# Sliding-window attention and MLP on one core: tables made on GpSimd, mask tables made later, the last block written in column halves

## The chip, the cores and the metric

The kernel runs on 1 core of one Trainium2 chip. The metric is the device time of one execution in microseconds (us). The times given for a kernel are the median of several runs.

## The reference

Inputs are q, k and v of shape (8 batches, 8 heads, 576 positions, 64) in float32, a gain of 512 values, and two weight matrices of 512 x 2048 and 2048 x 512. Cut to what matters, the reference computes:

```python
scores = q @ k.T / sqrt(64)
rel = pos[:, None] - pos[None, :]
mask = (rel >= 0) & (rel < 128)                 # causal, window of 128
scores = where(mask, scores - slope[head] * rel, -1e9)
x = softmax(scores) @ v                         # heads side by side: (8, 576, 512)
xn = (x - mean(x)) / sqrt(var(x) + 1e-6) * g    # over the 512 columns
out = x + relu(xn @ w_ch1) @ w_ch2
```

A softmax row is not shifted by its maximum in the kernel; the sum of the exponentials comes from a column of ones beside v.

## The kernel before

**Blocks and chunks.** The 8 x 576 rows are cut into 36 blocks of 128 rows. Two batches make a period of 9 blocks; block 4 of a period holds the end of one batch and the start of the next, and block 5 follows it. Each block sees itself and the block before it. Blocks are gathered into chunks (`CHUNKS`, L249: 2, 3, 3 and then seven of 4) for the MLP.

**Attention of a block** (L483 to L767): q, k and v are loaded on SP's queue (L360, or L436 for pairs of blocks, the "spans" starting at blocks 0, 2, 5 and 7, L280); q and k are cast to 16 bits (L498, or L530 for a span); they are transposed on TensorE (L563, L538) and copied out (L571, L552, L550), and from block 12 on by a DMA transpose (L578). Scores are computed into the PSUM banks `sc` (L599), ScalarE takes exp (L647), and the result is multiplied by a mask table that holds exp(-slope * distance) or 0 (L654). For blocks under `BY_BIAS` = 6 there is no multiply: TensorE first adds the bias to the scores with 8 matmuls per block of a scaled identity `sid` and a distance table `dist_t` (L615, the Z tasks). Then probabilities times v (L671, the pv tasks), a reciprocal and a multiply (L688, L692), the statistics (L709, L714), `xs` (L720), and its transpose: on TensorE (L732, copied out at L740 or L742) for blocks under `X_BY_DMA` = 13, by DMA (L747) after.

**Tables.** The identity, `dist_t` in its three kinds (ordinary, the block with a batch border, the block after it) and the gain row are loaded on ScalarE's queue (L377, L381, L385). `sid` is made from the identity on VectorE (L403). The mask tables `mreg` (8 instructions of ScalarE, L410), `mmix` and `mnew` (4 copies and 3 memsets on GpSimd, L420 to L427) are made once, behind the pv of block 1 (`TABLE_AFTER`, L278, and L829).

**MLP of a chunk** (L769 to L825): 16 A tasks of 4 matmuls each (L781, as many columns as the chunk has rows), a relu after each on ScalarE or VectorE (L793, L791), and for each block 4 B tasks of 4 matmuls of 512 columns (L807), then `ot` = B * rstd + x (L815) and the store on SP's queue (L823).

**Weights.** Eight transfers of 512 columns or rows, issued on GpSimd's queue (L474 for w1, L476 for w2). `W_AFTER` (L463) says behind which cast each is issued: entry `at` stands for block at // 3, and at % 3 for its q, k or v cast (for a block of a span, always the v cast). The relu rows of 4 A tasks need one w1 quarter.

**What sets the order.** Everything is a task with a list of what it depends on, an urgency `v` (smaller first), the engines that could take it with an assumed duration on each, and, for TensorE's work, the PSUM banks. `Plan.run` (L100 to L220) plays this forward in Python with the assumed durations and writes out a fixed instruction order for each engine. A wait is met on the chip, but the order stays. `SLACK` (L281) is a time that the planner adds between an end on another engine and TensorE's use of it (first value under 30 us, second after, third behind weight transfers). `PICK` (L282) says per task and block which engines are allowed; where two are, an engine leaves the task to the other if that one would end sooner (L166). For the multiply the assumed durations are VectorE 0.69 and GpSimd 1.4 us (L658); for the cast of a span GpSimd 1.25, ScalarE 1.06 and VectorE 0.65 us (L531). Where TensorE would be idle in the first `WARM` = 26 us of the plan, small filler matmuls on zeros are emitted (L839); until then they hold the fourth of the four PSUM banks `fb`. `LEAD` shifts how far attention runs ahead of the MLP.

Of the kernel before, what the change touches and what calls it, by code (L numbers as in the profile page):

```python
# [13 lines left out]
ALU = mybir.AluOpType  # L14
# [32 lines left out]
class Plan:  # L47
# [7 lines left out]
    BEGIN = 0.75  # L55
    LANDING = {"DMA SP": (0.7, 1.3), "DMA ACT": (0.7, 1.3), "DMA POOL": (1.6, 1.4)}
    LAST_OF_RUN = 1.0

    def __init__(self):
        self.tasks, self.rings, self.banks, self.opens = [], [], {}, {}  # L60
# [6 lines left out]
    def add(self, name, eng, emit, deps=(), v=0.0, lat=None, acq=None, rel=None):  # L67
        if not isinstance(eng, dict):
            eng = dict([eng])
        if lat is None:  # L70
            lat = 0.2 if "PE" in eng else 0.05 + max(self.OVERLAP.get(e, 0.0) for e in eng)
        eng = {e: c - self.OVERLAP.get(e, 0.0) for e, c in eng.items()}
        t = Task(name, eng, emit, deps, v, lat, acq, rel)
        self.tasks.append(t)
        return t

# [5 lines left out]
        i.room = d.room = room  # L82
        return i, d

    SLACK = (0.2, 0.2, 0)

    def slack(self, t, when):

# [11 lines left out]
    def run(self):  # L100
# [15 lines left out]
        heap, n = [], 0  # L116
        for t in self.tasks:
            if t.left == 0:
                heap.append((self.BEGIN, n, t))
                n += 1  # L120
        for x in self.opens.values():
            heap.append((x, n, None))
# [25 lines left out]
        while left:  # L148
            while heap and heap[0][0] <= now + 1e-9:
                t = heapq.heappop(heap)[2]  # L150
# [8 lines left out]
            for e in engines:  # L159
# [3 lines left out]
                for t in avail[e]:  # L163
# [8 lines left out]
                    ok, b = bank(t)  # L172
# [4 lines left out]
                t, b = best  # L177
# [11 lines left out]
                if t.rel is not None:  # L189
                    waits[t.rel] -= 1  # L190
                    if waits[t.rel] == 0:
                        p, hb = held[t.rel]
# [31 lines left out]
def kernel(  # L224
# [21 lines left out]
    PERIOD = 2 * S // P  # L246
    CB = 4
    CH = CB * P
    CHUNKS = [2, 3, 3, 4, 4, 4, 4, 4, 4, 4]  # L249
    FIRST = [sum(CHUNKS[:c]) for c in range(len(CHUNKS))]  # L250
    CHUNK_OF = [c for c, n in enumerate(CHUNKS) for _ in range(n)]
    VD = D + 2
# [5 lines left out]
    def head_of(bank, slot):  # L258
        return 2 * (2 * (bank // 2) + slot) + bank % 2

    kk = np.arange(P)[:, None]
    cc = np.arange(2 * P)[None, :]
    qq = cc % P
    rel = np.where(cc < P, cc + P, cc - P) - kk
    valid = (rel >= 0) & (rel < window)
    tail = np.where(cc < P, qq < HALF, (kk >= HALF) | (qq < HALF))
    head = (cc >= P) | (kk >= HALF)
    dist = np.stack([np.where(m, rel, 16000) for m in (valid, valid & tail, valid & head)], 1).astype(np.float16)
    dist_dram = nc.inline_tensor(dist, name="dist")
    iden_dram = nc.inline_tensor(np.eye(P, dtype=np.float16), name="iden16")  # L270

    pool = ctx.enter_context(tc.tile_pool(name="sb", bufs=1))
    psum = ctx.enter_context(tc.tile_pool(name="ps", bufs=1, space=bass.MemoryType.PSUM))

    SPAN = 36.0
    LEAD = 1.5
    WARM = 26.0
    TABLE_AFTER = 1  # L278
    SPLIT = 6
    SPANS = [0, 2, 5, 7]  # L280
    SLACK = (0.1, 0.4, 0.5)  # L281
    PICK = {('xt', 0): 'ACT DVE', ('xt', 8): 'ACT', ('cv', 5): 'POOL ACT', ('cv', 0): 'POOL', ('ev', 8): 'DVE', ('ev', 1): 'DVE', ('mkb', 8): 'DVE', ('mkb', 3): 'POOL', ('mka', 2): 'DVE', ('mkb', 4): 'POOL', ('ev', 3): 'ACT', ('mka', 0): 'DVE', ('ck', 8): 'ACT', ('mkb', 0): 'POOL', ('cq', 5): 'POOL', ('ev', 5): 'DVE', ('ck', 2): 'POOL', ('ck', 7): 'POOL ACT', ('mkb', 6): 'DVE', ('mka', 5): 'DVE', ('cq', 6): 'POOL ACT', ('cq', 2): 'POOL ACT', ('xt', 6): 'ACT DVE', ('mka', 7): 'DVE', ('cq', 8): 'ACT', ('xt', 5): 'DVE', ('mka', 6): 'POOL', ('cv', 7): 'POOL ACT', ('cv', 3): 'POOL', ('xt', 3): 'ACT DVE', ('mka', 4): 'POOL', ('mka', 3): 'POOL', ('ev00', 4): 'DVE', ('cs1', 1): 'POOL', ('cs0', 0): 'POOL ACT', ('ev10', 3): 'DVE', ('xt', 2): 'ACT', ('cq', 3): 'POOL', ('cs0', 8): 'POOL ACT', ('ev01', 8): 'DVE', ('ev10', 8): 'ACT', ('ev11', 5): 'ACT', ('cs0', 2): 'POOL ACT', ('cq', 4): 'POOL', ('ev00', 8): 'DVE ACT', ('ev01', 0): 'ACT', ('cv', 8): 'ACT', ('ev11', 0): 'ACT', ('cv', 4): 'POOL', ('mkb', 5): 'POOL', ('ev01', 6): 'DVE', ('cv', 6): 'ACT', ('ev10', 5): 'DVE ACT', ('cs1', 4): 'POOL ACT', ('ev', 0): 'ACT', ('cv', 2): 'POOL ACT', ('ev00', 2): 'ACT', ('ev00', 7): 'ACT', ('ev10', 2): 'DVE'}  # L282
    BY_BIAS = 6
    MASK_AT = 6
    QK_BY_DMA = 12
    X_BY_DMA = 13

    plan = Plan()
    plan.SLACK = SLACK

    def sb(name, shape, dt):
        return pool.tile(shape, dt, tag=name, name=name)
# [47 lines left out]
    def av(i, stage=0.0):  # L340
        return (i / CB - LEAD) * SPAN + stage

# [31 lines left out]
    for t in vx.tiles:  # L374
        nc.vector.memset(t[:, :, D:VD], 1.0)

    d_iden = plan.transfer("iden", "ACT", 0.5, 0.15, 0.0, lambda e, b: nc.scalar.dma_start(out=iden, in_=iden_dram.ap()), (), -1e6)[1]  # L377
    d_dist = [
        plan.transfer(
            f"dist{n}", "ACT", 0.5, 0.25 * (k1 - k0), 0.0,  # L380
            lambda e, b, k0=k0, k1=k1: nc.scalar.dma_start(out=dist_t[:, k0:k1, :], in_=dist_dram.ap()[:, k0:k1, :]), deps, v,  # L381
        )[1]
        for n, k0, k1, deps, v in ((0, 0, 1, (), -9e5), (1, 1, 3, (), av(2, 0.0)))
    ]
    d_row = plan.transfer("g", "ACT", 0.5, 0.02, 0.0, lambda e, b: nc.scalar.dma_start(out=g_row[:, :], in_=moe_g_ln.unsqueeze(0)), (), -8e5)[1]  # L385

# [14 lines left out]
    for h in range(H):  # L401
        def emit(e, b, h=h):
            nc.vector.tensor_scalar(out=sid[:, h, :], in0=iden[:, :], scalar1=-float(slopes[h] / inv_sqrt_d), scalar2=None, op0=ALU.mult)  # L403
# [3 lines left out]
    for bank in range(4):  # L407
        for slot in range(2):
            def emit(e, b, bank=bank, slot=slot):
                nc.scalar.activation(  # L410
                    out=mreg[:, bank, slot, :], in_=dist_t[:, 0, :], func=AF.Exp,
                    scale=-float(slopes[head_of(bank, slot)]),
                )
            tm.append(add(f"mreg{bank}{slot}", ("ACT", 0.4), emit, [d_dist[0]], av(MASK_AT, 0.0)))
    tmix, tnew = [], []
    for dst, lst, name in ((mmix, tmix, "mmix"), (mnew, tnew, "mnew")):
        vv = av(MASK_AT, 0.0)
        for hb in range(2):
            def emit(e, b, dst=dst, hb=hb):
                nc.gpsimd.tensor_copy(dst[:, 2 * hb : 2 * hb + 2, :, :], mreg[:, 2 * hb : 2 * hb + 2, :, :])  # L420
            lst.append(add(f"{name}c{hb}", ("POOL", 1.2), emit, tm, vv))
    def z1(e, b):
        nc.gpsimd.memset(mmix[:, :, :, HALF:P], 0.0)
    def z2(e, b):
# [35 lines left out]
            load("v", v, v32, i, vl + 0.02),  # L460
        )

    W_AFTER = [11, 13, 14, 14, 17, 18, 18, 22]  # L463
    t_w = {}

    def weights(i, casts):
# [16 lines left out]
    def attention(i):  # L483
# [142 lines left out]
        for halves in ((0,), (1,)) if i < SPLIT else ((0, 1),):  # L626
            tag = "ab"[halves[0]] if i < SPLIT else ""
            acq = [(f"sc{hf}", f"S{i}{hf}") for hf in halves]
            part = len(halves) / 2
            z_ = []  # L630
            if bias:
                z_ = [add(f"Z{tag}{i}", ("PE", (0.87 if r else 0.46) * part), e_z(halves), t_sid + [d_dist[kind > 0]], av(i, 1.5 + 0.6 * halves[0]), acq=acq)]
            st_ = add(f"S{tag}{i}", ("PE", 0.19 + (0.45 if r else 0.23) * part), e_s(halves), z_ + qkt_done[i] + prev, av(i, 2.0 + 0.6 * halves[0]), acq=acq)
            qkt.reads(i, st_)
            if r:
                qkt.reads(i - 1, st_)
            for half in halves:
                s_[half] = st_
# [130 lines left out]
    def mlp(c):  # L769
# [26 lines left out]
            relu.append(r_)  # L796
        for j in range(nb):
            i = FIRST[c] + j
            key = f"B{i}"
            last = None  # L800
            for f0 in range(0, NFB, 4):
                vm = v0 + 16 * per + (4 * j + f0 / 4) * SPAN / 32

                def e_b(e, b, j=j, f0=f0, key=key):
                    pm = fb[plan.held[key][1]]
                    for f in range(f0, f0 + 4):
                        nc.tensor.matmul(  # L807
                            pm[:, :], ht[c][:, f, j * P : j * P + P], w2sb[:, f, :],
                            start=(f == 0), stop=(f == NFB - 1),
                        )  # L810
                last = add(f"{key}.{f0}", ("PE", 0.864), e_b, relu[f0 : f0 + 4] + [t_w[4 + f0 // 4][1], last], vm, acq=("fb", key))
                ht.reads(c, last)

            def e_o(e, b, i=i, j=j, key=key):
                nc.vector.scalar_tensor_tensor(  # L815
                    out=ot[i][:, :], in0=fb[plan.held[key][1]][:, :], scalar=rstd[c][:, j : j + 1],
                    in1=xb[i][:, :], op0=ALU.mult, op1=ALU.add,
                )
            o = add(f"o{i}", ("DVE", 0.75), e_o, [last, kept[c]], vm - 4.0, rel=key)
            ot.writes(i, o); rstd.reads(c, o); xb.reads(i, o)  # L820

            def e_d(e, b, i=i):
                nc.sync.dma_start(out=out_flat[i * P : i * P + P, :], in_=ot[i][:, :])  # L823
            t, d = plan.transfer(f"out{i}", "SP", 0.42, 0.8, 0.12, e_d, [o], vm - 4.0)
            ot.reads(i, d)  # L825

    for i in range(NBLK):
        attention(i)
        if i == TABLE_AFTER:  # L829
            for t in tm:  # L830
                t.deps.append(pv_done[i])
    for c in range(len(CHUNKS)):
        mlp(c)

# [45 lines left out]
```

The softmax here doesn't subtract the row's maximum and nothing guards it: scores larger than these inputs give would overflow.

## Time and profile before

| what | value |
|---|---|
| time, median of 7 runs | 324.61 us (323.83 to 325.96) |
| the profiled execution's own time | 324.12 us |
| its span, first to last instruction | 322.3 us |
| TensorE busy | 314.3 us, 2640 matmuls, of them 138 fillers |
| VectorE, ScalarE, GpSimd busy | 181.4, 162.6 and 79.7 us |
| granted TensorE clock | 1.00 over the whole span |
| moved by DMA | 51.91 MB |

The profile is that of one execution. "L781" is line 781 of the kernel. PE is TensorE's matmuls, PEld its weight loads, DVE VectorE, ACT ScalarE, POOL GpSimd, SP the engine that issues most DMAs; a q behind an engine's name is its queue of issuing instructions. In a timeline, a row gives the start, the time from there to the end of the last instruction merged into it, the engine, the line, the operation, what it writes and reads, and in square brackets how long the engine had been idle and what released it. Matmuls overlap in the pipeline, so the time that a matmul adds is read from the distance between starts, not from its duration.

### The profile page before, as it was taken

How to read it: one execution, taken by the hardware profiler on the slowest of the kernel's cores; microseconds unless marked ns; L12 is line 12 of the kernel's file. 1: busy time of each engine (PE TensorE's matmuls, PEld its weight loads, DVE VectorE, ACT ScalarE, POOL GpSimd, SP SyncE). 2: the span in 40 equal slices, each digit the busy share in tenths (PEclk: the TensorE clock that was granted, in tenths of full speed). 3: DMA queues.
4: the chain of work that ended last, by engine and by line, in shares of the span. 5: the costliest groups of instructions: out<-in, count | busy, mean ns of one | idle time of the engine just before them, and what ended most of it. 6: DMA issues, size and time to landing. Idle time of an engine off the chain costs nothing.

```text
span 322.3 us, 6669 instructions
## 1 busy us (share of the span) xinstructions
PE 314.3 (98%) x2640; PEld 171.9 (53%) x2640; DVE 181.4 (56%) x398; ACT 162.6 (50%) x264; POOL 79.7 (25%) x116
## 2 busy tenths in 40 slices
PE   8989999999999999999999999999999999999994
PEld 6877775556644554554454444444444444444441
DVE  1289189677610696695397496566756675321011
ACT  2798897134704950683277434752475247305500
POOL 2379272354202420620340260160000000000000
PEclk9999999999999999999999999999999999999999
DMA  8999999999999996999999899984420220011011
GB/s 203 237 214 217 244 200 214 215 200 268 224 198 260 206 189 132 243 218 208 177 221 197 179 169 254 229 164 116 114 49 18 83 82 18 17 67 65 0 66 65
DMA packets 151921, 51.91 MB, mean 161 GB/s; under 512 B 134737, under 2 KB 147281, under 8 KB 151890
## 3 DMA queue, kind: packets, MB, share of 16 engines
q1 hardware_dynamic: 147232, 47.07, 69.7%
q0 software_dynamic: 4224, 4.19, 7.8%
q8 instruction: 20, 0.33, 0.5%
q10 hardware_dynamic: 434, 0.23, 0.3%
q14 instruction: 11, 0.09, 0.1%
HBM read 36.93 MB, written 9.44 MB: 144 GB/s over the span
## 4 chain that ended last, share of the span: by engine, by line
PE 85%; DMA 5%; SPq 4%; DVE 3%; issue 1%; ACT 0%; POOL 0%; DVEq 0%; POOLq 0%
PE fb L807 38%; PE fb L781 37%; PE sc L599 5%; PE fb L671 4%; DMA w1sb<-in_moe_w_ch_dram 3%; SPq L360 3%; SPq L436 1%; DMA k<-in_k_dram 1%; DVE probs L654 1%; DVE st L709 1%; PE fb L732 1%; DVE xs L720 0%; PE fb L563 0%; DVE xb L692 0%; DVE xt L740 0%
## 5 line engine op out<-in xcount | busy, mean ns | idle before, releaser
L781 PE MATMUL fb<-xt,w1sb 128*128 128x512 f16 (+2 forms) x640 | 135.5, 358 | 0.7 <-DVE xt L740 0.3
L807 PE MATMUL fb<-w2sb,ht 128*128 128x512 f16 x576 | 132.5, 379 | 0.0
L793 ACT ACTIVATE ht<-fb 128x512 f16<-128x512 f32 (+2 forms) x142 | 78.9, 557 | 77.9 <-PE fb L781 76.6
L647 ACT ACTIVATE probs<-sc 128x1024 f16<-128x1024 f32 (+1 forms) x72 | 67.5, 976 | 42.8 <-PE sc L599 42.8
L781 PEld LDWEIGHTS <-w1sb 128*128 128x128 f16 x640 | 59.3, 98 | 54.9 <-issue 0.6
L807 PEld LDWEIGHTS <-ht 128*128 128x128 f16 x576 | 54.0, 98 | 60.7 <-issue 0.2
L815 DVE SCALAR_TENSOR_TENSOR ot<-fb,rstd,xb 128x512 f32<-128x512 f32 x36 | 27.0, 749 | 59.2 <-PE fb L807 52.2
L654 DVE TENSOR_TENSOR probs<-probs,mreg 128x1024 f16<-128x1024 f16 (+1 forms) x47 | 33.1, 712 | 20.7 <-ACT probs L647 20.5
L512 POOL CAST vx<-v 128x512 f16<-128x512 f32 x33 | 20.8, 633 | 87.4 <-PE fb L671 61.1
L498 POOL CAST qk<-q 128x512 f16<-128x512 f32 x28 | 19.3, 691 | 57.2 <-DMA qkt<-qk 46.7
L671 PEld LDWEIGHTS <-probs 128*128 128x128 f16 x544 | 24.4, 97 | 12.8 <-issue 1.3
L692 DVE TENSOR_TENSOR xb<-fb,rec 128x256 f16<-128x256 f32 x72 | 29.9, 421 | 1.7
L720 DVE SCALAR_TENSOR_TENSOR xs<-xb,mv,g_t 128x512 f16<-128x512 f16 x36 | 28.3, 787 | 2.8 <-DMA xt<-xs 1.9
L671 PE MATMUL fb<-vx,probs 128*128 128x65 f16 x544 | 27.2, 193 | 1.0 <-DVE qkt L550 0.9
L688 DVE RECIPROCAL rec<-fb 128x4 f32<-128x4 f32 x72 | 12.2, 175 | 24.9 <-PE fb L671 24.6
L709 DVE BATCH_NORM_STATS2 st<-xb 128x6 f32<-128x512 f16 x36 | 24.9, 692 | 1.0
L498 POOL CAST qk<-k 128x512 f16<-128x512 f32 x28 | 19.5, 698 | 6.9 <-DMA k<-in_k_dram 4.2
L599 PEld LDWEIGHTS <-qkt 64*128 64x128 f16 x544 | 15.3, 94 | 10.7 <-issue 9.1
L599 PE MATMUL sc<-qkt 64*128 64x128 f16 x288 | 19.6, 216 | 0.1
L791 DVE TENSOR_SCALAR ht<-fb 128x512 f16<-128x512 f32 (+2 forms) x18 | 10.8, 605 | 15.3 <-PE fb L781 14.5
L599 PE MATMUL sc<-qkt,qkt 64*128 64x128 f16 x256 | 18.3, 219 | 0.0
L839 PE MATMUL fb<-warm_t 128*128 128x128 f16 x138 | 11.1, 245 | 1.0 <-DVE warm_t L371 1.0
(47 smaller groups left out, 115.5 us busy)
## 6 DMA issues: line engine op xcount, KB each, us to landing
out_dram<-ot SPq DMA_DIRECT2D x36, 256.0 KB, 2.5
v<-in_v_dram SPq DMA_DIRECT2D x32, 256.0 KB, 4.9
q<-in_q_dram SPq DMA_DIRECT2D x24, 256.0 KB, 5.1
k<-in_k_dram SPq DMA_DIRECT2D x24, 256.0 KB, 4.9
qs<-in_q_dram SPq DMA_DIRECT2D x4, 512.0 KB, 6.1
ks<-in_k_dram SPq DMA_DIRECT2D x4, 512.0 KB, 7.9
w1sb<-in_moe_w_ch_dram POOLq DMA_DIRECT2D x4, 512.0 KB, 10.9
w2sb<-in_moe_w_ch_dram POOLq DMA_DIRECT2D x4, 512.0 KB, 8.8
```

What stands on the lines that cost most here:

```text
L498: en.tensor_copy(out=qk16[nrm[i]][:, a, :], in_=s)
L599: nc.tensor.matmul(scs[half][:, g, c0 : c0 + P], kt[rows, 1, hp, :], qkt[i][rows, 0, hp, :], start=not bias, stop=True, skip_group_check=True,
L647: nc.scalar.activation(out=o, in_=n_, func=AF.Exp, scale=inv_sqrt_d)
L654: en.tensor_tensor(out=pv, in0=pv, in1=mask[:, 2 * half : 2 * half + 2, :, lo:], op=ALU.mult)
L671: nc.tensor.matmul(pp[:, hh * (D + 1) : hh * (D + 1) + D + 1], probs[i][:, bank, slot, side * P : side * P + P], vx[i - 1 + side][:, h, 0 ...
L692: nc.vector.tensor_tensor(out=xb[i][:, 256 * half : 256 * half + 256].rearrange("p (h d) -> p h d", d=D), in0=pp[:, :, 0:D], in1=rec[2 * i ...
L709: nc.vector.bn_stats(out=st[i][:, :], in_=xb[i][:, :])
L720: nc.vector.scalar_tensor_tensor(out=xs[i][:, :], in0=xb[i][:, :], scalar=mv[c][:, j, 0:1], in1=g_t[:, :], op0=ALU.subtract, op1=ALU.mult,)
L781: nc.tensor.matmul(fb[b][:, 0:n_], w1sb[:, kb, f * P : f * P + P], xt[c][:, kb, 0:n_], start=(kb == 0), stop=(kb == NKB - 1),)
L793: nc.scalar.activation(out=ht[c][:, f, 0:n_], in_=src, func=AF.Relu)
L807: nc.tensor.matmul(pm[:, :], ht[c][:, f, j * P : j * P + P], w2sb[:, f, :], start=(f == 0), stop=(f == NFB - 1),)
L815: nc.vector.scalar_tensor_tensor(out=ot[i][:, :], in0=fb[plan.held[key][1]][:, :], scalar=rstd[c][:, j : j + 1], in1=xb[i][:, :], op0=ALU. ...
```

## The change

All of it is in one function and the planner above it.

1. The identity and `dist_t` are no longer loaded but made on GpSimd (memset, iota, affine_select, copies). The gain row is still loaded.
2. `mreg` is made behind the pv of block 3 instead of block 1, and `mmix` and `mnew` behind that of block 4.
3. `BY_BIAS` goes from 6 to 5: block 5 is masked by the multiply instead of the Z matmuls. `X_BY_DMA` goes from 13 to 14, so block 13's `xs` is transposed on TensorE instead of by DMA.
4. The last chunk of 4 blocks becomes one of 3 and one of 1. Block 35's B is done in two column halves, each in a PSUM bank, with its own `ot` instruction and store.
5. `W_AFTER`, `SPLIT`, `LEAD`, `WARM`, `SLACK` and `MASK_AT` get other values, `PICK` gets an entry for nearly every task of blocks 0 to 11, and `PRI` and `HOLD` are new: an amount added to a task's urgency, and an earliest time for it in the plan.

Of `PICK`, these entries matter below. The casts of the first span, `('cs0', 0)` and `('cs1', 0)`, go from "POOL ACT" (and GpSimd by default) to "POOL DVE". The multiplies of a block's two halves (`mka`, `mkb`) are allowed on GpSimd alone for block 5 (first half) and blocks 6, 8 and 11 (both halves): 7 instructions. Before, from block 6 on, only the first half of block 6 was; VectorE does all others.

```diff
-    SLACK = (0.2, 0.2, 0)
+    SLACK: tuple = (0, 0.4, 0)
...
-    CHUNKS = [2, 3, 3, 4, 4, 4, 4, 4, 4, 4]
+    CHUNKS = [2, 3, 3, 4, 4, 4, 4, 4, 4, 3, 1]
...
-    LEAD = 1.5
-    WARM = 26.0
-    TABLE_AFTER = 1
-    SPLIT = 6
+    LEAD = 1.7
+    WARM = 20.0
+    TABLE_AFTER = 3
+    MIX_AFTER = 4
+    SPLIT = 4
...
-    SLACK = (0.1, 0.4, 0.5)
+    SLACK = (0.1, 0.3, 0.4)
...
+    PRI = {'mka7': -7.4, 'T9': -24.7, 'k11.i': 0.8, 'v4.i': 5.2, 'B2.0': -1.2, 'v5.i': 8.4, 'Sa0': -9.2}
+    HOLD = {'S9': 59.97, 'Zb2': 14.76, 'rc1.3': 20.0, 'dist': 1.4, 'G': 4.27, 'ck9': 49.72, 'eT0.10': 8.66, 'rs2': 51.44, 'pva2': 19.78}
-    BY_BIAS = 6
-    MASK_AT = 6
+    BY_BIAS = 5
+    MASK_AT = 5
...
-    X_BY_DMA = 13
+    X_BY_DMA = 14
...
+    d_iden = pool_do("iden1", 0.2, [], -1e6, lambda en: en.memset(iden[:, :], 1.0))
+    d_iden = pool_do("iden2", 0.3, [d_iden], -9e5, keep(iden[:, :], iden[:, :], 0, 1, -1, 0.0, ALU.is_equal))
+    t = pool_do("dist", 0.35, [], -8e5, lambda en: en.iota(
+        dist_t[:, 0, :].rearrange("p (s c) -> p s c", s=2), pattern=[[-P, 2], [1, P]], base=P, channel_multiplier=-1,
+        allow_small_or_imprecise_dtypes=True,
+    ))
+    t = [
+        pool_do("dist00", 0.3, [t], -7e5, keep(dist_t[:, 0, 0:P], dist_t[:, 0, 0:P], -1, 1, -1, far)),
+        pool_do("dist01", 0.3, [t], -7e5, keep(dist_t[:, 0, P:], dist_t[:, 0, P:], 0, -1, 1, far)),
+    ]
+    d_dist = [t, [
+        pool_do("dist1", 0.35, t, av(2, -8.0), lambda en: en.tensor_copy(dist_t[:, 1, :], dist_t[:, 0, :])),
+        pool_do("dist2", 0.35, t, av(2, -8.0), lambda en: en.tensor_copy(dist_t[:, 2, :], dist_t[:, 0, :])),
+    ]]
+    d_dist[1] += [
+        pool_do("dist1a", 0.2, d_dist[1][0:1], av(2, -7.0), lambda en: en.memset(dist_t[:, 1, HALF:P], far)),
...
-    W_AFTER = [11, 13, 14, 14, 17, 18, 18, 22]
+    W_AFTER = [6, 8, 11, 17, 20, 21, 26, 27]
...
+            cuts = (0, d_model // 2, d_model) if i == NBLK - 1 else (0, d_model)
+            for c0, c1 in zip(cuts, cuts[1:]):
+                key = f"B{i}" if c1 - c0 == d_model else f"B{i}.c{c0}"
...
+                                pm[:, 0 : c1 - c0], ht[c][:, f, j * P : j * P + P], w2sb[:, f, c0:c1],
...
+                o = add(f"o{i}.{c0}", ("DVE", 0.2 + 0.55 * (c1 - c0) / d_model), e_o, [last, kept[c]], vm - 4.0, rel=key)
...
+                    nc.sync.dma_start(out=out_flat[i * P : i * P + P, c0:c1], in_=ot[i][:, c0:c1])
...
-        if i == TABLE_AFTER:
-            for t in tm:
-                t.deps.append(pv_done[i])
+        for at, tables in ((TABLE_AFTER, tm), (MIX_AFTER, mixes)):
+            if i == at:
+                for t in tables:
+                    t.deps.append(pv_done[i])
```

## The prediction

> **What bounds the kernel now.** I read the page's busy rows and chain first, then TensorE's timeline over the first 60 us, then GpSimd's and ScalarE's over the same stretch, and the end of the chain last.
>
> ```profile
> PE 314.3 (98%) x2640; PEld 171.9 (53%) x2640; DVE 181.4 (56%) x398; ACT 162.6 (50%) x264; POOL 79.7 (25%) x116
> ...
> PE 85%; DMA 5%; SPq 4%; DVE 3%; issue 1%; ACT 0%; POOL 0%; DVEq 0%; POOLq 0%
> ```
>
> TensorE is the bound, and the chain leaves it for DMA, SP and VectorE only at the start. In the table by stretches it is busy for 258.08 of the 258.12 us from 60 us to the last matmul. So a change gains by taking matmuls away, by shortening the start, or by shortening what follows the last matmul. But "busy" counts fillers (L839), so the start has to be read row by row:
>
> ```profile
> 6.36 1.09 PE L388 MATMUL fb<-ot,ot 1*128 1x512 f32 x2 [0.57 <-DMA ot<-in_moe_g_ln_dram]
> 7.39 0.62 PE L615 MATMUL sc<-dist_t,sid 128*128 128x128 f16 x8
> 7.84 1.33 PE L839 MATMUL fb<-warm_t 128*128 128x128 f16 x21
> 9.02 0.61 PE L538 MATMUL fb<-iden,qs 128*128 128x128 f16 x8
> 9.46 1.22 PE L839 MATMUL fb<-warm_t 128*128 128x128 f16 x19
> 10.53 0.61 PE L538 MATMUL fb<-iden,ks 128*128 128x128 f16 x8
> 10.97 0.94 PE L839 MATMUL fb<-warm_t 128*128 128x128 f16 x14
> 11.98 0.40 PE L599 MATMUL sc<-qkt 64*128 64x128 f16 x8
> ...
> 18.66 0.40 PE L671 MATMUL fb<-vx,probs 128*128 128x65 f16 x8 [0.90 <-DVE qkt L550]
> ...
> 31.01 0.61 PE L781 MATMUL fb<-xt,w1sb 128*128 128x256 f16 x4 [0.32 <-DMA w1sb<-in_moe_w_ch_dram]
> ```
>
> From start to start, the time given to fillers or waits after 7.84 us is 1.18 + 1.07 + 1.01 + 0.70 + 0.50 + 1.12 + 0.96 + 0.38 (the rows of x8, x5, x1, x17 and x5 fillers that are not shown), and 0.30 and 0.32 of waits near 29 and 31 us: 7.54 us. Before 7.84 us there is only the gain row and one Z, 1.5 us of work, so 6.3 us are dead. After 31 us TensorE hardly waits.
>
> Why is it not fed? The casts in front of the first transposes:
>
> ```profile
> 5.04 1.04 POOL L530 CAST qs<-qs 128x1024 f16<-128x1024 f32 x1 [4.59 <-DMA qs<-in_q_dram]
> 7.12 1.04 POOL L530 CAST ks<-ks 128x1024 f16<-128x1024 f32 x1 [1.04 <-DMA ks<-in_k_dram]
> ```
>
> q's cast ends at 6.08 and its transposes start at 9.02; k's ends at 8.16 and they start at 10.53. So 2.9 and 2.4 us of the start are lost in the written order (fillers, the gain matmul and Z stand ahead in TensorE's queue), not to a late input. Later the inputs are late: DMA's share is 1.12 from 7.84 to 32.30 us, the second span's k is cast at 14.73, and the second w1 quarter, issued at 20.45 behind k's cast of block 4, lands at 31.0.
>
> **The change part by part.**
>
> *Tables on GpSimd.* Removed are three loads on ScalarE's queue, 32 + 64 + 128 KB:
>
> ```profile
> dist_t<-dist ACTq DMA_DIRECT2D x1, 128.0 KB, 5.2
> dist_t<-dist ACTq DMA_DIRECT2D x1, 64.0 KB, 4.0
> iden<-iden ACTq DMA_DIRECT2D x1, 32.0 KB, 2.3
> ```
>
> At the 203 GB/s of the first 7.84 us, 224 KB are 1.1 us of DMA that the first span's and its followers' loads get back. The gain row moves from third to first on its queue (issued at 1.68 before). Added before the first Z are five GpSimd instructions (a memset and a compare for the identity, an iota and two compares for the distances). No row shows an iota or an affine_select. Ends: 0.11 us (memset of one column) and 2.12 us (the longest GpSimd row). Nearest by size is the 512-column memset, 0.52; for 128 to 256 columns I take 0.35, so 5 x 0.35 = 1.75 from 0.45, ready at about 2.3 to 2.5 (`HOLD` puts the iota at 1.4 or later), and `sid` 0.9 later. Nothing asks for them before about 6 us: the cover is 2.8 us, or a mean of 0.9 us an instruction with `sid` behind. Beyond that, Z of block 0 holds up the transposes behind it in TensorE's queue; at 2.12 us each it is 5 x 2.12 + 0.45 + 0.9 = 11.95, or some 6 us late. Ends 0 and +6, taken 0. The five copies and memsets of the other two kinds lie in GpSimd's idle time before 14 us (4.17 us idle ahead of the cast at 14.73).
>
> The GPSIMD Engine Reference of the Trainium skill, 2.1 Instruction dispatch, speaks against this part: the first call into freshly loaded GpSimd code costs some 6 us, and no instruction in the profile shows it. The row that bears on it is GpSimd's only multiply: two pool-configuration entries stand at 43.0 and 43.1 and the multiply runs at 44.20, released by ScalarE, so what is seen is 1.1 us or less. With the rule's 6 us ahead of the iota, an estimate from that page, the tables would be ready near 8 us and the sum smaller by some 2 us; with the row, by nothing.
>
> *Span casts of block 0 on VectorE.* Removed: two GpSimd casts of 1.04. VectorE's price is bounded by its 1024-column 16-bit multiply, 0.75, and twice its 512-column float32 `tensor_scalar`, 2 x 0.69 = 1.37; I take 1.0. VectorE idles 9.84 us ahead of 13.85, so it is covered. The worth is in the plan, which assumed 1.25 and now 0.65, and so puts the transposes earlier.
>
> *Mask tables later.* ScalarE is busy 7.52 of 8 us from 16 to 24 us, eight `mreg` instructions of 0.42 (3.3 us) among its exps. They move behind the pv of block 3 (24.8 us). GpSimd's copies (1.05 x 2 + 1.27 x 2) and memsets (0.52 + 0.52 + 0.94), 6.6 us, move behind the pv of block 4 (27.8 us). Now block 5 needs `mnew`; its scores ran at 40.0, its pv at 42.3. So 6.6 us plus two casts fit; should block 5 come at 34, the cover is gone and its multiply waits 0 to 2 us, with A matmuls of chunks 0 and 1 before it.
>
> *w1 earlier, w2 later.* Quarters 0 and 1 go behind block 2's v cast (16.05) instead of 18.06 and 20.45: 2 and 4 us earlier; quarter 2 behind block 3's (17.50 against 22.53); quarter 3 behind block 5's v cast instead of 24.24. w2's last one goes behind block 9's q cast, which stood at 50.77, against 47.03: 3.7 us later, near 60 us where B's fourth group ran (59.65). No room there, no loss by the rows.
>
> *The start, summed.* The dead 7.54 us can fall to 0 at best and the first 6.3 by some 1.5 (the transposes cannot precede the landing at 5.04). At the least only the 1.1 us of DMA come back, or nothing if the wait just changes its name. I take half of 7.54, since the written order wastes 5 us by itself while the DMA queue stays over-full: **-3.8**.
>
> *TensorE's work.* Block 5's Z matmuls go: 2 x 0.44 (26.52 to 26.95, 28.07 to 28.51), -0.87. Block 13's four transposes come: 4 x 0.056, +0.22. **-0.65**. On VectorE and GpSimd come two multiplies, beside other work.
>
> *Last chunk of 3 and 1.* A: 64 x 0.2157 = 13.81 becomes 64 x 0.162 + 64 x 0.056 = 13.95; B of block 35 becomes 32 x 0.1087 = 3.48 for 3.45; **+0.2**. The small relus (0.28 by the 0.107 us step between 256, 384 and 512 columns) alternate on two engines against 0.22 of A each, with four banks: 0 to +1, taken **+0.1**.
>
> *The tail.*
>
> ```profile
> 304.27 13.83 PE fb L807 x64
> 318.12 0.75 DVE ot L815
> ```
>
> From the last matmul to the end are 4.2 us. Half the columns take 0.28 less (VectorE's relu: 0.69, 0.55, 0.43 at 512, 384, 256 columns). The store is 128 instead of 256 KB: loads of these sizes landed 0.5 to 1.2 us apart in a busy queue; ends 0 and -0.5, taken -0.15. **-0.43**.
>
> *Multiplies on GpSimd.* Seven instead of one:
>
> ```profile
> 44.20 2.12 POOL L654 TENSOR_TENSOR probs<-probs,mreg 128x1024 f16<-128x1024 f16 x1 [1.12 <-ACT probs L647]
> ```
>
> The plan assumes 1.4, so each is 0.72 late, and where both halves of a block are there (6, 8, 11) the second is 1.44 late. Behind it in TensorE's fixed order stand pv and all MLP matmuls. The one row had its pv at 46.95, 0.63 after its end, so it cost nothing; `SLACK` falls by 0.1. Ends 0 and 7 x 0.72 = +5.0; I take 0.4 for each of three blocks, **+1.2**, nearer to the row.
>
> The SBUF — State Buffer page of the Trainium skill, Who interferes with whom, adds that a VectorE instruction with two SBUF inputs and a GpSimd one that reads SBUF shut each other out. The VectorE multiply that began at 45.99, before this GpSimd one ended, took 0.89 against a mean of 0.75: 0.14 more. By the rule up to 7 x 2.12 us of such VectorE work would wait; by the row 1 us, and VectorE is 56% busy.
>
> Sum: -3.8 - 0.65 + 0.3 - 0.43 + 1.2 = **-3.4**. The profiled execution, 322.3 of span and 1.8 around it, would go from 324.12 to 320.7. It lies 0.5 under the median, so from the median: 324.61 - 3.4 = **321.2**.
>
> **Rivals.** (1) *Forecast*: the start shortens by 2 to 7 us; 317.5 to 323.0. (2) *The start is fixed by DMA*: the transposes come earlier, but the loads of blocks 2 to 4 and w1 still land when they did, and the saved time returns as waits on k or w1. For it: DMA share 1.12 there. Against: the 2.9 and 2.4 us, and 224 KB less. Then only -0.65 + 0.3 - 0.43 = -0.8: 323.8. (3) *Slower, by GpSimd's multiplies*: late pv in blocks 5 to 11 stall TensorE for the full 5.0, with half of the start's gain: -1.9 - 0.8 + 5.0 = +2.3, 326.9. With the forecast's start it decides once a multiply costs more than (3.8 + 0.8) / 7 = 0.66 us of TensorE, with half of it 2.7 / 7 = 0.39. For it: 2.12 against 1.4. Against: the one row cost nothing.
>
> **How the numbers follow.** Chances: forecast 0.64, DMA 0.16, multiplies 0.20. A measurement of this kernel tells about 0.3% (1 us) from no change. Faster (under 323.6): 0.64 + 0.06 = 0.70. Same: 0.10 of the second and 0.03 of the third, 0.13. Slower (over 325.6): 0.17. The range is 317.4 to 326.4: the forecast's own low end, the second case whole, and the third up to a stall of 4.5 us.
>
> **What would show it.** Right: first transposes near 6 to 7 us, scores of block 0 near 9, fewer than 60 fillers after them, w1's second quarter landed before 29, last matmul near 315, tail near 3.8. Wrong: TensorE waits on `mask` products or GpSimd at L671 between 35 and 75 us adding up to over 2; a Z waiting on GpSimd before 9 us; the same waiting under the names of k or w1.

## The result, and the profile after

The changed kernel takes 328.02 us (median of 13 runs, 326.94 to 333.17) against 324.46 for the kernel before (34 runs): a ratio of 1.0112, 95% interval 1.0089 to 1.0135. It is 3.6 us slower, where 3.4 us faster was forecast. The profiled execution took 327.78 us with a span of 326.1.

The page of the changed kernel, busy time and chain:

```profile
PE 314.8 (97%) x2687; PEld 175.4 (54%) x2687; DVE 182.0 (56%) x397; ACT 171.0 (52%) x292; POOL 87.6 (27%) x121
...
PE 82%; DVE 12%; DMA 1%; ACT 1%; POOL 1%; issue 1%; SPq 0%; DVEq 0%
```

TensorE's share fell from 98 to 97%, and 12% of the chain now runs over VectorE, where it was 3%. To see where, I took every matmul's distance to the next start and subtracted the time that it needs at full clock (512 columns 0.216 us and so on); fillers count as lost altogether.

| lost on TensorE, us | before | after |
|---|---|---|
| up to 32.3 us | 13.9 | 14.4 |
| 32.3 to 60 | 0.8 | 2.8 |
| 60 to 80 | 0.2 | 0.2 |
| 80 to 100 | -0.1 | 1.3 |
| after 100 | 0.4 | 0.9 |

That is +4.4 us; of the 0.5 after 100 us, 0.46 is one wait on VectorE at 123 us. TensorE's work fell by 0.36, and the time after the last matmul from 4.42 to 4.14. Together +3.76, and the span grew by 3.73.

The start of TensorE's timeline, after the change (start, time, row; the fillers are L859):

```profile
3.17 1.06 PE L632 MATMUL sc<-dist_t,sid 128*128 128x128 f16 x8
4.03 2.12 PE L859 MATMUL fb<-warm_t 128*128 128x128 f16 x20
6.08 1.12 PE L404 MATMUL fb<-ot,ot 1*128 1x512 f32 x2
...
7.37 0.61 PE L555 MATMUL fb<-iden,qs 128*128 128x128 f16 x8
7.82 1.50 PE L859 MATMUL fb<-warm_t 128*128 128x128 f16 x24
10.16 0.62 PE L555 MATMUL fb<-iden,ks 128*128 128x128 f16 x8 [0.84 <-DVE ks L547]
```

q's transposes came 1.65 us earlier (7.37 for 9.02), k's only 0.37. VectorE's timeline says why: the k cast stands behind a copy of q's transposed values, which waits for ScalarE's copy of their other half (8.02 to 8.77).

```profile
5.01 0.69 DVE L547 CAST qs<-qs 128x1024 f16<-128x1024 f32 x1 [2.49 <-DMA qs<-in_q_dram]
8.80 0.73 DVE L567 COPY qkt<-fb 128x512 f16<-128x512 f16 x1 [3.09 <-ACT qkt L569]
9.43 0.68 DVE L547 CAST ks<-ks 128x1024 f16<-128x1024 f32 x1
```

The largest new waits later, in TensorE's timeline, are for GpSimd's products:

```profile
48.33 0.41 PE L688 MATMUL fb<-vx,probs 128*128 128x65 f16 x8 [0.39 <-POOL probs L671]
...
82.17 0.42 PE L688 MATMUL fb<-vx,probs 128*128 128x65 f16 x8 [1.20 <-POOL probs L671]
```

GpSimd's timeline and, below it, VectorE's: while a pair of products runs on GpSimd, an xs of VectorE takes 2.0 us instead of 0.75.

```profile
44.07 4.20 POOL L671 TENSOR_TENSOR probs<-probs,mreg 128x1024 f16<-128x1024 f16 x2
...
53.23 4.22 POOL L671 TENSOR_TENSOR probs<-probs,mreg 128x1024 f16<-128x1024 f16 x2 [0.61 <-ACT probs L664]
```

```profile
46.83 2.00 DVE L737 SCALAR_TENSOR_TENSOR xs<-xb,mv,g_t 128x512 f16<-128x512 f16 x1
...
55.91 2.09 DVE L737 SCALAR_TENSOR_TENSOR xs<-xb,mv,g_t 128x512 f16<-128x512 f16 x1
```

The end, in VectorE's timeline: two instructions of 256 columns stand where one of 512 took 0.75. The second, the only one behind the last matmul, takes 0.48.

```profile
321.75 0.93 DVE L834 SCALAR_TENSOR_TENSOR ot<-fb,rstd,xb 128x256 f32<-128x256 f32 x2 [5.29 <-PE fb L826]
```

### The profile page after: what moved, and what is told of

Same layout as the page of the kernel before. It is cut to its first block, busy times and chain, and to the rows that moved or that the text cites. A ratio compares the mean times of both kernels' runs of the same rounds, so it can differ in the third digit from the quotient of the medians.

```text
span 326.1 us, 6798 instructions
## 1 busy us (share of the span) xinstructions
PE 314.8 (97%) x2687; PEld 175.4 (54%) x2687; DVE 182.0 (56%) x397; ACT 171.0 (52%) x292; POOL 87.6 (27%) x121
## 4 chain that ended last, share of the span: by engine, by line
PE 82%; DVE 12%; DMA 1%; ACT 1%; POOL 1%; issue 1%; SPq 0%; DVEq 0%
PE fb L798 35%; PE fb L826 35%; PE sc L616 4%; PE fb L688 4%; DVE xs L737 3%; DVE xb L709 2%; PE fb L859 2%; DVE st L726 2%; DVE probs L671 2%; DMA v<-in_v_dram 1%; DVE qkt L567 1%; ACT qkt L569 1%; PE fb L555 1%; POOL probs L671 1%; PE sc L632 1%
## 5 line engine op out<-in xcount | busy, mean ns | idle before, releaser
L798 PE MATMUL fb<-xt,w1sb 128*128 128x512 f16 (+3 forms) x704 | 134.5, 340 | 0.4
L826 PE MATMUL fb<-w2sb,ht 128*128 128x512 f16 (+1 forms) x592 | 134.1, 373 | 0.0
L810 ACT ACTIVATE ht<-fb 128x512 f16<-128x512 f32 (+3 forms) x159 | 81.7, 519 | 85.7 <-PE fb L798 84.8
L798 PEld LDWEIGHTS <-w1sb 128*128 128x128 f16 x704 | 64.0, 98 | 55.2 <-issue 0.9
L834 DVE SCALAR_TENSOR_TENSOR ot<-fb,rstd,xb 128x512 f32<-128x512 f32 (+1 forms) x37 | 27.0, 732 | 67.0 <-PE fb L826 55.0
L671 DVE TENSOR_TENSOR probs<-probs,mreg 128x1024 f16<-128x1024 f16 (+1 forms) x42 | 28.1, 683 | 16.2 <-ACT probs L664 16.0
L737 DVE SCALAR_TENSOR_TENSOR xs<-xb,mv,g_t 128x512 f16<-128x512 f16 x36 | 31.7, 882 | 0.9
L515 POOL CAST qk<-q 128x512 f16<-128x512 f32 x26 | 17.2, 660 | 48.6 <-DMA qkt<-qk 33.4
L515 POOL CAST qk<-k 128x512 f16<-128x512 f32 x25 | 18.2, 730 | 4.6 <-DMA k<-in_k_dram 4.6
L671 POOL TENSOR_TENSOR probs<-probs,mreg 128x1024 f16<-128x1024 f16 x6 | 13.1, 2198 | 4.8 <-ACT probs L664 4.8
```

The lines of the kernel that those rows point to most:

```text
L515: en.tensor_copy(out=qk16[nrm[i]][:, a, :], in_=s)
L671: en.tensor_tensor(out=pv, in0=pv, in1=mask[:, 2 * half : 2 * half + 2, :, lo:], op=ALU.mult)
L737: nc.vector.scalar_tensor_tensor(out=xs[i][:, :], in0=xb[i][:, :], scalar=mv[c][:, j, 0:1], in1=g_t[:, :], op0=ALU.subtract, op1=ALU.mult,)
L798: nc.tensor.matmul(fb[b][:, 0:n_], w1sb[:, kb, f * P : f * P + P], xt[c][:, kb, 0:n_], start=(kb == 0), stop=(kb == NKB - 1),)
L810: nc.scalar.activation(out=ht[c][:, f, 0:n_], in_=src, func=AF.Relu)
L826: nc.tensor.matmul(pm[:, 0 : c1 - c0], ht[c][:, f, j * P : j * P + P], w2sb[:, f, c0:c1], start=(f == 0), stop=(f == NFB - 1),)
```

## The experiments

The theory: the multiplies on GpSimd are late for TensorE and hold up VectorE. The first rival: the start, written more tightly than the chip runs it. The second: the changed kernel's order as a whole. Since every edit of a setting makes the planner write another order, all but one of the kernels keep the order of their base and change only what is issued in a place (the three with another last chunk keep it up to that chunk). Ratios are to the kernel before, with 95% intervals; the changed kernel stands at 1.0112.

### The multiplies

```diff
+            if t.name[:3] in ("mka", "mkb") and e == "POOL": e = "DVE"
             if t.emit is not None:
```

> The changed kernel with its plan and its written order kept; only the seven mask multiplies of blocks 5, 6, 8 and 11 that it gives to GpSimd are issued on VectorE, in their place. Theory 'late multiplies': the three stalls of TensorE behind GpSimd products (0.15 near 46.3, 0.57 near 48.3 and 1.36 near 82.2 us, 2.1 us together) go, and some of the waits on xs behind them; 1.8 to 2.8 us less than the changed kernel, so some +1 to +1.7 us over the kernel before. Rival 'VectorE is full there': seven times 0.75 us more on VectorE between 36 and 80 us return as waits on xs and on the relus; less than 0.7 us gained.

1.0036 (1.0000 to 1.0073). The waits on GpSimd are gone, and the gain, 2.5 us by the ratios, is in the range forecast. But between 40 and 48 us TensorE still loses 1.65 us, now to VectorE: 0.64 and 0.95 from start to start at L798, most likely for a PSUM bank that VectorE has not emptied.

```profile
44.70 1.25 PE L798 MATMUL fb<-xt,w1sb 128*128 128x384 f16 x8 [0.48 <-DVE xb L709]
...
46.99 0.60 PE L798 MATMUL fb<-xt,w1sb 128*128 128x256 f16 x4 [0.80 <-DVE mv L731]
```

The reverse in the order of the kernel before:

```diff
+            if t.name in ("mka6", "mkb6", "mka8", "mkb8", "mka11", "mkb11"): e = "POOL"
             if t.emit is not None:
```

> The kernel before with its plan and written order kept; only five more mask multiplies (second half of block 6, both halves of blocks 8 and 11) are issued on GpSimd, in their place. Theory 'GpSimd's multiplies': each is 1.4 us longer than on VectorE, pv waits for them at L671, and VectorE instructions with two SBUF inputs that run beside them stretch (xs from 0.75 to about 2); 1.5 to 4 us slower than before. Rival 'the written order of the changed kernel is what fails, not the engine': under 0.7 us slower.

1.0117 (1.0066 to 1.0169): five multiplies cost as much as the whole change. TensorE waits 3.3 us for GpSimd's products, nearly all of it at the second halves of blocks 6 and 11:

```profile
49.35 0.42 PE L671 MATMUL fb<-vx,probs 128*128 128x65 f16 x8 [1.54 <-POOL probs L654]
```

```profile
87.13 0.42 PE L671 MATMUL fb<-vx,probs 128*128 128x65 f16 x8 [1.56 <-POOL probs L654]
```

Why VectorE stretches, in the changed kernel again:

```diff
+            if t.name[:3] in ("mka", "mkb") and e == "POOL":
+                half, blk = "ab".index(t.name[2]), int(t.name[3:])
+                for _ in range(2):
+                    nc.gpsimd.memset(probs[blk][:, 2 * half : 2 * half + 2, :, :], 0.01)
+                continue
             if t.emit is not None:
```

> The changed kernel with its order kept; each of the seven mask multiplies on GpSimd is replaced by two memsets of the same tile, some 2.1 us together, which write SBUF and read nothing. The mask is left out in those half blocks. Theory 'VectorE is shut out while GpSimd reads': xs near 46.8 and 55.9 us falls from 2.0 to about 0.8 and the multiply near 41.4 from 1.8 to 0.7 us; TensorE's waits on xs and on a relu near 48.9, 56.6 and 58.1 us (1.0 us together) go, its waits on GpSimd's products stay; 0.6 to 1.6 us less than the changed kernel. Rival 'GpSimd is just late': the stretched VectorE instructions have another cause and stay; within 0.4 us.

1.0022 (0.9997 to 1.0046), 2.9 us less than the changed kernel by the ratios, more than forecast. Two memsets take 1.93 to 1.97 us together, some 0.2 less than a multiply, and TensorE's waits for them, which I expected to stay, fell from 1.6 to 0.4 us; so the run does not divide the gain between the multiplies' being late and their shutting VectorE out. What it does show is the xs beside them:

```profile
46.27 0.75 DVE L737 SCALAR_TENSOR_TENSOR xs<-xb,mv,g_t 128x512 f16<-128x512 f16 x1
...
54.42 0.75 DVE L737 SCALAR_TENSOR_TENSOR xs<-xb,mv,g_t 128x512 f16<-128x512 f16 x1
```

GpSimd was busy with the memsets over both (43.45 to 47.31 and 51.96 to 55.82 us), but it read nothing, and xs was back at 0.75. So it is GpSimd's reading that shuts VectorE's two-input instruction out.

### The start

```diff
-        for _ in range(int((b - a - 0.06) / 0.06)):
+        for _ in range(int((b - a - 0.06) / (0.107 if b < 6.0 else 0.06))):
```

> The changed kernel with its order kept; fillers before 6 us of the plan are counted at 0.107 us each, as they run there, instead of 0.06, so there are some 17 fewer. Theory 'the start is lost in the written order': the first transposes move from 7.4 to about 6.2 us and the whole start with them, 1.0 to 1.5 us less than the changed kernel. Rival 'loads decide the start': the first transposes are earlier, but those of the second span (15.1) and of block 4 (22.9) stay within 0.3 us, and the time within 0.4 us.

1.0091 (1.0059 to 1.0123): no gain that can be told from the changed kernel. The surprise is in its timeline: with fewer fillers TensorE stayed at half its rate past 10 us.

```profile
4.54 2.07 PE L404 MATMUL fb<-ot,ot 1*128 1x512 f32 x2
...
6.73 1.06 PE L555 MATMUL fb<-iden,qs 128*128 128x128 f16 x8
```

Both rows took 1.12 and 0.61 us in the changed kernel. k's transposes came at 10.14, as late as ever.

```diff
+            if t.name == "cT0.1": e = "POOL"
             if t.emit is not None:
```

> The changed kernel with its order kept; only the first span's cast of k is issued on GpSimd, which is idle there, instead of on VectorE, where it stands behind a copy that waits for the transposes of q. Theory 'the start is lost in the written order': the cast starts near 7 instead of 9.43 us, k's transposes start near 8.6 instead of 10.16, and 1.0 to 1.6 us of the total go. Rival 'loads decide the start': k's transposes move, those of the second span and of block 4 do not, and the time stays within 0.4 us.

1.0094 (1.0064 to 1.0124). Here the transposes of k did come 1.5 us earlier (8.65), those of the second span too (13.60 for 15.13), and of block 4 (21.15 for 22.90). Some 0.5 us of the 1.5 are fillers that came to full rate earlier in this execution. It brought nothing. Of the lead, 1.75 us at block 4, some 1.1 were gone by 27 us, in waits for block 4's k cast, which itself waited for its load, and on xs. The last 0.6 us went at 57 us into a wait for a quarter of w2:

```profile
57.19 1.02 PE L826 MATMUL fb<-w2sb,ht 128*128 128x512 f16 x4 [0.75 <-DMA w2sb<-in_moe_w_ch_dram]
```

That quarter was issued at 48.65 us, behind a pair of GpSimd's multiplies; with the multiplies on VectorE it was issued at 43.50. So the two losses are not independent, and an earlier k together with the multiplies on VectorE was not run. My rival had the result right and its reason only in part: the second span did move.

Tables alone, in the order of the kernel before (`make_iden` and the others are the instructions of the diff in the front, issued where the loads were):

```diff
-lambda e, b: nc.scalar.dma_start(out=iden, in_=iden_dram.ap())
+make_iden
...
-lambda e, b, k0=k0, k1=k1: nc.scalar.dma_start(out=dist_t[:, k0:k1, :], in_=dist_dram.ap()[:, k0:k1, :])
+make_dist1 if n else make_dist0
```

> The kernel before with its plan and written order kept; only the identity and the distance tables are made on GpSimd instead of loaded. Theory 'the tables themselves help a little': 224 KB less in the first 8 us bring the k of the first span some 0.5 to 1 us earlier and the k of the second span by as much; 0.3 to 1.0 us faster than before. Rival 'GpSimd's tables cost': the first casts on GpSimd wait behind them; 0.3 to 1 us slower. If neither, within 0.3 us: the loss of the changed kernel lies wholly in its order.

0.9989 (0.9954 to 1.0024). All transposes up to block 4's come 1.06 to 1.08 us earlier, but not because q and k land earlier. GpSimd's timeline has their casts at 5.15 and 6.99 us, where they were at 5.04 and 7.12:

```profile
5.15 1.04 POOL L545 CAST qs<-qs 128x1024 f16<-128x1024 f32 x1 [1.68 <-DMA qs<-in_q_dram]
6.99 1.04 POOL L545 CAST ks<-ks 128x1024 f16<-128x1024 f32 x1 [0.81 <-DMA ks<-in_k_dram]
```

The lead is there already at the gain row's matmul (5.27 for 6.36). Of it, 0.57 are the wait for the gain row, now first on its queue. The other 0.52 are the 48 fillers ahead of it (4.27 us for 4.79), whose full rate began at 4.0 instead of 5.1 us in that execution. At 26 us all is lost again, and VectorE's and GpSimd's timelines show to whom:

```profile
23.45 2.71 DVE L735 SCALAR_TENSOR_TENSOR xs<-xb,mv,g_t 128x512 f16<-128x512 f16 x1
```

```profile
24.14 1.05 POOL L435 COPY mmix<-mreg 128x1024 f16<-128x1024 f16 x1
25.12 0.74 POOL L489 DMA_DIRECT2D w1sb<-in_moe_w_ch_dram  x1
```

An xs of 0.75 us took 2.71 beside GpSimd's copies of the mask tables, and TensorE lost 1.8 us to it. GpSimd's reading instructions cover some 1.4 us of its time, so 0.6 of the 1.96 us that it lost are not explained by them.

So I moved those copies to where GpSimd is idle, with and without the tables on GpSimd (both in the order of before):

```diff
+            if t.name[:5] in ("mmixc", "mnewc") or t.name in ("z1", "z2", "z3"):
+                late.append((t.emit, e, b))
+                continue
+            if late and t.start > 86.0:
+                for x in late:
+                    x[0](*x[1:])
+                late = []
```

> The kernel before with its plan and written order kept; the identity and distance tables made on GpSimd, and the mix mask tables (four copies and three memsets on GpSimd), which nothing reads before 110 us, made at 86 us of the plan, where GpSimd is idle, instead of 23 to 32 us. Theory 'the 1.07 us that the tables bring are lost where xs stretches beside GpSimd's copies': the xs of 2.7 us near 23.5 falls under 1.2, the wait of 1.8 us near 26.2 goes, and the kernel is 0.8 to 1.8 us faster than before. Rival 'loads of w1 decide': the wait on xs goes but comes back as one on w1 near 30 us; within 0.4 us of before.

0.9969 (0.9943 to 0.9995), faster by an interval that just leaves out 1 (this is the late mix kernel below). The long xs is gone; 0.4 us of waiting for w1 appears near 31 us, so the rival is right about a part.

> The kernel before with its plan and written order kept; only the mix mask tables are made at 86 us of the plan instead of 23 to 32 us, the identity and distance tables are still loaded. Theory 'VectorE is shut out while GpSimd reads': the xs near 27.3 falls from 1.57 to 0.75 us and the wait of 0.46 us near 29 goes; 0.2 to 0.8 us faster than before, less than with the tables on GpSimd. Rival: no gain, within 0.2 us.

0.9997 (0.9978 to 1.0015): no gain that can be told. Its wait on xs went too, but one for a q cast came near 30 us.

The other direction, the changed kernel with its tables loaded (the three loads on ScalarE's queue in place of the GpSimd instructions):

> The changed kernel with its order kept; only the identity and the distance tables are loaded on ScalarE's queue again instead of made on GpSimd. Theory 'the tables are not the loss': the loads of the first span land 0.5 to 1.1 us later, part of it is absorbed by 32 us; 0 to 1.0 us slower than the changed kernel. Rival 'GpSimd's tables cost something': 0.3 us or more faster than the changed kernel.

1.0224 (1.0150 to 1.0298), far outside what I expected: 3.6 us slower than the changed kernel. Z of block 0 stands first in its order:

```profile
7.15 1.01 PE L643 MATMUL sc<-dist_t,sid 128*128 128x128 f16 x8 [3.83 <-DMA dist_t<-dist]
```

TensorE idled 3.8 us, stayed at half rate, and began q's transposes at 12.6. In this order the tables must be early.

### Block 5 and the order

The changed kernel, all multiplies on VectorE, block 5 by bias matmuls again:

```diff
         def e_s(halves):
             def emit(e, b):
+                if i == BY_BIAS:
+                    e_z(halves)(e, b)
...
-                                    start=not bias,
+                                    start=i > BY_BIAS,
...
+            if t.name in ("mka5", "mkb5"):
+                continue
```

> The changed kernel with its order kept, all mask multiplies on VectorE as in the first experiment, and in addition block 5 masked as in the kernel before: its bias matmuls stand right ahead of its scores and its two multiplies are left out. Theory 'VectorE is full where block 5 to 8 now need their masks': of the 1.6 us of waits on VectorE between 40 and 48 us at least 1.0 go and TensorE gets 0.87 of bias matmuls; 0.1 to 0.9 us less than the first experiment. Rival 'the bias matmuls cost what they always did': the waits stay and 0.5 to 0.9 us are added.

1.0079 (1.0045 to 1.0112), 0.43% or 1.4 us over the first experiment. The waits of 0.47 and 0.96 us stayed and the bias matmuls were added, as the rival had it; 0.5 us of the two profiles' difference is an earlier start in the first one.

The same part alone in the order of before (bias matmuls of block 5 left out, two multiplies on VectorE where its exps end):

```diff
+            if t.name in ("Za5", "Zb5"):
+                continue
+            while due and t.start >= due[0][0]:
+                due.pop(0)[1]()
             if t.emit is not None:
                 t.emit(e, b)
+            if t.name in ("exa5", "exb5"):
+                due.append((t.end, plan.more[t.name]))
```

> The kernel before with its plan and written order kept; only block 5 is masked by two multiplies on VectorE behind its exps, and its bias matmuls (0.87 us of TensorE near 27 us) are left out. Theory 'VectorE is full there': the 0.87 us come back as waits on VectorE between 42 and 50 us; within 0.4 us of before. Rival 'TensorE's work decides': 0.5 to 0.9 us faster than before.

1.0053 (1.0021 to 1.0084), slower by 1.7 us, more than my theory said. TensorE's waits, in us, times and longest:

```profile
PE fb L673 <- DVE probs L654: 1.1, 2, 0.8
PE fb L734 <- DVE xs L722: 1.1, 2, 0.9
```

There are 0.87 us of TensorE's work less, but 1.5 us are lost near 44 us behind VectorE's multiplies (the first took 1.63 beside a GpSimd cast), and 1.05 for 0.46 near 29 us on an xs, ahead of which the bias matmuls had stood as cover.

The one kernel with a new order, the changed one told the price:

```diff
-pick("mk" + "ab"[half], "DVE", DVE=0.69 if r else 0.42, POOL=1.4 if r else 0.8)
+pick("mk" + "ab"[half], "DVE", DVE=0.69 if r else 0.42, POOL=2.2 if r else 1.1)
```

> The changed kernel with one number of its plan changed: a multiply on GpSimd is assumed at 2.2 us (1.1 for a half one) instead of 1.4, near the 2.1 to 2.2 that it takes. The plan makes a new order from it. Theory 'the settings pay only under the wrong price': the waits on GpSimd's products go, but TensorE waits elsewhere; as slow as the changed kernel or slower, 327.5 to 334. Rival 'only the lateness hurt': 2 us or more under the changed kernel, 326 or less.

1.0242 (1.0193 to 1.0290), 332.8 us. With the price near the measured one, these settings make a worse order, so they do not repair the price by themselves. That the settings were found under the wrong price is an inference and not shown.

### What stood up, put together

The late mix kernel with the last chunk and the column halves of the diff:

> The kernel before with its settings; identity and distance tables on GpSimd, the mix tables made at 86 us, and the last chunk of 3 and 1 with block 35 in column halves. Expected from the parts: the late mix kernel with tables was 0.3% faster than before, the tail measured 4.14 instead of 4.42 us in the changed kernel's profile and TensorE's work grows by 0.2; 0.5 to 1.3 us faster than before. If the tail's parts cost more than they bring, under 0.4 us faster.

0.9929 (0.9896 to 0.9961), median 322.97 (12 runs): faster than both kernels. After the last matmul it takes 3.52 us, for 4.17 in the late mix kernel. The rest of its lead over that kernel (0.9969) is at least in part scatter: their orders are the same up to the last chunk, and yet this profile is 1.03 us ahead at 7 us, where its fillers came to full rate earlier, and 1.9 us ahead at 133 us.

```diff
+            if t.name == "w1.i":
+                continue
             if t.emit is not None:
                 t.emit(e, b)
+            if t.name == "w0.i":
+                t_w[1][0].emit(e, b)
```

> The kernel just above, with w1's second quarter issued right behind the first (some 2.5 us earlier) instead of behind block 4's cast of k. Theory 'the start ends with w1's second quarter': the wait of 0.54 us near 31 us on it goes and 0.3 to 0.8 us more are gained. Rival 'the loads share one limit': block 4's k lands later by as much, its transposes and scores move back, and the time is the same or up to 0.5 us longer.

0.9966 (0.9933 to 0.9998): nothing gained by an earlier w1. Its profile is 1.03 us behind the one above at the gain row's matmul (7.14 for 6.11), again by the fillers' rate, and still 1.03 behind at the last matmul.

Tables, tail, late mix for the border blocks only, and block 5 as in its own experiment:

> The kernel before with its settings; tables on GpSimd, the last chunk of 3 and 1 with block 35 in column halves, the mix table of the border blocks made at 86 us and that of the blocks behind them where it was, and block 5 masked by multiplies on VectorE without bias matmuls. If the parts add: 0.9 to 1.5% faster than before (the late mix and tail gave 0.7%, bias matmuls 0.87 us). If VectorE is full near 45 us: the same 0.7% as without the last part, or less.

0.9984 (0.9953 to 1.0015). The parts do not add. TensorE loses 1.3 us near 44 us to block 5's multiplies and as much between 21 and 29 us to xs, one of which took 1.41 beside the copies of the table that block 5 now needs early; which of the two takes back more is not shown.

## Why the prediction was wrong, point by point

Two terms of the sum failed. The start, put at -3.8 on the ground that the written order alone wastes 5 us, gave nothing. The multiplies on GpSimd, put at +1.2 from a row that had waited for nothing, cost 2.1 to 2.5 us. Of the rest, the 1.2 us that remain with all multiplies on VectorE stay open.

- **The start, -3.8: wrong, +0.5 us.** I took half of the dead time because "the written order wastes 5 us by itself". The 6.3 us ahead of it, which I called dead, were not all order either: 0.57 were a wait for the gain row's load, and the fillers there ran at half rate up to 5.1 us. The first transposes did come earlier, but the k cast, written behind a copy on VectorE, did not, and the k cast on GpSimd showed that even a 1.5 us lead through block 4 is used up: by a load and by VectorE's chain of xs and copies (3.97 of 4 us busy from 24 to 28 in the changed kernel, 3.93 before), and by w2 at 57 us. I had seen only the loads.
- **Multiplies on GpSimd, +1.2: mis-sized.** There are 2.1 us of direct waits, and 2.5 us by the ratio go when they move to VectorE (1.0112 to 1.0036). I bounded it by 5.0 and priced it by one row, whose pv happened to stand far behind. Put into the order of before, five cost 3.8 us.
- **VectorE shut out: the row was misread.** The Trainium skill's SBUF — State Buffer page, Who interferes with whom, says that a VectorE instruction with two SBUF inputs and a GpSimd one that reads SBUF exclude each other. I set against it the multiply that took 0.14 us more. That multiply began at 45.99, when GpSimd's had 0.33 us to run, so it could lose no more than 0.33. The stretched xs (2.0, 2.09 and 2.71 us) and the memset experiment bear the page out, but for the 0.6 us of the third that GpSimd's reading does not cover. The row that I misread, in VectorE's timeline of the kernel before:

```profile
45.99 0.89 DVE L654 TENSOR_TENSOR probs<-probs,mreg 128x1024 f16<-128x1024 f16 x1
```

- **Block 5 without bias matmuls, -0.65 with its neighbour: right as work, wrong as time.** TensorE's work fell by 0.36 with the last chunk's +0.2, where 0.45 was reckoned. "Beside other work" was wrong: VectorE was 6.77 of 8 us busy from 40 to 48 us in the kernel before, and the part alone costs 1.7 us.
- **Tables: right that they cost nothing, wrong in what they bring.** The GpSimd instructions took 0.20, 0.29, 0.34, 0.31 and 0.34 us (0.35 assumed). But the 1.1 us of DMA did not reach the first loads: with the tables alone, q's cast came 0.11 later, k's 0.13 earlier and the next ones 0.5 to 0.6 earlier. The 6 us that the Trainium skill's GPSIMD Engine Reference, 2.1 Instruction dispatch, gives for a first call are not seen: the pool-configuration entries stand at 0.96 and 0.99 us, the first compare runs at 1.09 and the iota at 1.35.
- **Tail, -0.43: -0.28 in these two profiles, and about right over all.** The last instruction is 0.27 shorter, and its store landed 1.79 us after it instead of 2.06. What follows the landing took 1.60 instead of 1.41 us here, but it varies from 0.97 to 1.60 between the profiles. The time after the last matmul is 4.24 us on average in the six without column halves and 3.77 in the eleven with them.
- **w2 later, no loss: right in the profile of the changed kernel,** though there is no room. Its second quarter landed at 56.46 us for a matmul at 56.88; with fewer fillers 1.5 us of waits on w2 appeared near 58 and 62 us, with the k cast on GpSimd 0.75 at 57.

The third rival, slower by GpSimd's multiplies, named the mechanism and 326.9 us; I gave it 0.20. That its number came near is luck: it holds a gain of 1.9 us at the start, which was not there, and 5.0 us of stalls, twice what was seen. The low end of the forecast, 317.5, was reckoned from the profiled execution; from the median it is 318.0. Left open: what holds the last 1.2 us of the first experiment. VectorE being full near 45 us fits; no kernel settles it.

## What to carry to other kernels

An engine that looks idle is no free place for an instruction if the busy one beside it is shut out while it reads: price a move to GpSimd by what VectorE loses while GpSimd reads, and by the reader's place in the fixed order, not by GpSimd's own time. When a lead at the start is forecast, look for what stands next in its way: an engine that is full when the start ends, a load, a transfer that is issued behind other work. Between the late mix kernel and the one with the tail, in one written order, a lead of 1.03 us lasted. And a row that disagrees with a rule is to be checked for how long the two instructions really ran side by side.

## What the runs showed of the hardware beyond that

TensorE's full rate begins at a time that differs between executions. The late mix kernel, and the one with the tail, issue the same instructions there; here are their fillers, in TensorE's timelines:

```profile
1.07 5.30 PE L854 MATMUL fb<-warm_t 128*128 128x128 f16 x48 [1.07 <-DVE warm_t L360]
```

```profile
1.07 4.58 PE L856 MATMUL fb<-warm_t 128*128 128x128 f16 x48 [1.07 <-DVE warm_t L360]
```

They went from one per 0.107 us to one per 0.056 after 5.95 and 4.57 us, and the first transposes came at 9.29 and 8.26. In fifteen of the seventeen profiles the step came between 3.9 and 6.0 us. Single profiles of this kernel thus differ by 1 us at the start. In the other two it came after 10 us: in the one with fewer fillers, and in the one where TensorE idled 3.8 us. Each of these is a single profile, so what delayed it there is not shown.
